# Second products as single matmuls between parts of the seven products, in a pattern of its own in each chunk

## The chip, the core and the metric

The kernel runs on one core of a Trainium2 chip. The metric is the device time of one execution in microseconds, and the median of several executions is compared. TensorE (PE) multiplies; VectorE (DVE), ScalarE (ACT) and GpSimd (POOL) do the element-wise work; SyncE (SP) issues most of the DMAs.

## The reference

Attention over a sliding window with a bias that grows with distance, and on its output, as rows of a 4608 x 512 matrix, a network of two layers with a squared ReLU between them.

```python
scores = scale * np.matmul(q, k.transpose(0, 1, 3, 2))       # 8 batches, 8 heads, 576 positions, 64 wide
mask = (rel >= 0) & (rel < 128)
scores = np.where(mask, scores + bias[None], -1000000000.0)
attn = np.exp(scores - max); attn = attn / (sum + 1e-09)
x = np.matmul(attn, v) as (4608, 512)
h = np.maximum(x @ w_in, 0.0)                                # w_in 512 x 2048
out = h * h @ w_out                                          # w_out 2048 x 512
```

## The kernel before

The 4608 rows of x go in nine chunks `c` of 512, and the 2048 hidden columns in 16 blocks `f` of 128. Matrix products keep their precision in three single-pass matmuls per operand pair: high part by high part, low by high, high by low.

The **first product** (x by `w_in`) is done plainly in chunks 0 and 1 (`gemm1`, line L224 of the profile). From chunk 2 on, two blocks of `f` at a time make one **step** `n` (eight steps a chunk, steps 16 to 71), by Strassen's scheme in Winograd's form: **seven products** M1, M5, M6, M2, M7, M3, M4 in this order (`seven`, `product`, L319), each of six matmuls 256 wide. M1, M6, M7 and M4 build up in one PSUM bank (`chain`), M5, M2 and M3 in another (`rest`). Between them stand **drains**, which copy or add a partial sum out of PSUM into `four`: s1, R, s2 and C21 on ACT, C11, C22 and C12 on DVE. A product waits for the drain of the one before it in its bank (`BEHIND`). Their left operands, `flow`, are sums of weights that were written to DRAM once, and come back by DMA two steps ahead; their right operands are parts of x (`xu`) and sums of such parts (`tees`). After a step, `squared` makes the hidden values on DVE (`r` or `spare`), ACT rounds them to the high part `hh`, and DVE subtracts for the low part `hl`.

The **second product** (h by `w_out`, `part`, L376) takes for each `f` four **blocks** `m`, of three matmuls 512 wide: weight high by `hh`, weight high by `hl`, weight low by `hh`. They build up in four banks `acc` over the 16 blocks of `f` of a chunk; then `give` copies a bank to SBUF (L382, ACT or DVE) and `send` writes it out (L386). The blocks of a step are worked off one step later, from a list `blocks`.

The attention of a later chunk runs beside this. Every second step ends with a **visit** (L719 and L732): PE multiplies the probabilities of one pair of heads with v, and makes the scores of the next pair. Then ACT copies the scores (L613, L620), DVE masks them and finds the maxima (L632, L636, L400), ACT exponentiates (L407), DVE sums (L414, L415), POOL normalizes (L419), DVE transposes in squares (L471), two DMA passes finish the transposition (`pp` to `way` and back), and POOL cuts the squares at the window (L484); the next visit waits for that. DVE, ACT and POOL also turn the visit's result into `xu`, `lows` and `tees` (L669, L699, L704).

`middle` writes PE's order by hand, step after step. The other engines' order is made by `Plan`: each piece of work has an engine, an assumed duration, what it comes after, and a due time; `run` goes through time, and among the pieces of an engine that are ready it takes the one due first. `start` plans the part before, chunks 0 and 1's attention and chunk 0's products, in the same way. The order of all queues is fixed when the kernel is built.

In `middle`, a step before the change runs so: M1, two blocks, M5, M6, two blocks, M2, M7, then two blocks in odd steps or one in even ones, M3, M4, in odd steps the visit, and then three blocks in odd steps or two in even ones (in the last chunk always two blocks, and no visits):

```python
counts = (2, 2, 2, 3 if n % 2 else 2) if n % 2 or n >= FULL - 8 else (2, 2, 1, 2)
for names, count in zip((("M1",), ("M5", "M6"), ("M2", "M7"), ("M3", "M4")), counts):
```

Of the kernel before, what the change touches and what calls it, by code (L numbers as in the profile page):

```python
# [22 lines left out]
NF = DF // 128  # L23
NCC = DM // 128
NCH = B * S // 512
# [6 lines left out]
WAIT = 0.1  # L32
# [7 lines left out]
FIRST = 19  # L40
# [23 lines left out]
class Kern:  # L64
# [249 lines left out]
    def product(self, n, i, to, name, start=False):  # L314
        todo = []
        for (wh, wl), (xh, xl) in zip(self.operand(n, i), self.halves(n // 8, name)):
            todo += [(wh, xh), (wl, xh), (wh, xl)]
        for k, (w, x) in enumerate(todo):
            self.nc.tensor.matmul(to, w, x, start=start and k == 0, stop=k == 5, skip_group_check=True)  # L319

    def seven(self, n):
        nc, four = self.nc, self.four
        one, two = slice(0, 256), slice(256, 512)
        add = lambda to, x: nc.vector.tensor_tensor(to, to, x, op=ALU.add)  # L324
        return {
            "M1": lambda: (self.chain(), self.product(n, 0, self.P, "B11", True)),
            "s1": lambda: nc.scalar.copy(four[0][:, one], self.P),
            "M5": lambda: (self.rest(), self.product(n, 1, self.R, "T1", True)),
            "R": lambda: nc.scalar.copy(four[1][:, two], self.R),
            "M6": lambda: self.product(n, 2, self.P, "T2"),  # L330
            "s2": lambda: nc.scalar.copy(four[0][:, two], self.P),
            "M2": lambda: self.product(n, 3, self.Q, "B21"),
            "C11": lambda: add(four[0][:, one], self.Q),
            "M7": lambda: self.product(n, 4, self.P, "T3"),
            "C22": lambda: add(four[1][:, two], self.P),
            "M3": lambda: self.product(n, 6, self.R, "B22"),
            "C12": lambda: add(four[0][:, two], self.R),
            "M4": lambda: self.product(n, 5, self.P, "T4"),
            "C21": lambda: nc.scalar.copy(four[1][:, one], self.P),  # L339
        }  # L340
# [27 lines left out]
    def part(self, c, f, m):  # L368
        if f == 0 and m == 0:
            self.acc = self.start_banks if c == 0 else [None] * 4  # L370
        if f == 0 and c:
            self.acc[m] = self.ac.tile([128, 512], F32, name="acc")
        hh, hl = self.h[c, f] if m < 3 else self.h.pop((c, f))
        wl, wh = self.block(1, f, m)
        for i, (w, h) in enumerate(((wh, hh), (wh, hl), (wl, hh))):
            self.nc.tensor.matmul(self.acc[m], w, h, start=(f == 0 and i == 0), stop=(f == NF - 1 and i == 2))  # L376
        if f == NF - 1:
            self.full[c, m] = self.acc[m]

    def give(self, c, m):  # L380
        o = self.out[c, m] = self.op.tile([128, 512], F32, name="o")
        (self.nc.scalar.copy if m % 2 else self.nc.vector.tensor_copy)(o, self.full.pop((c, m)))  # L382

    def send(self, c, m):
        out = self.outd[m * 128 : m * 128 + 128, 512 * c : 512 * c + 512]
        (self.nc.scalar if c == NCH - 1 and m == 3 else self.nc.sync).dma_start(out, self.out.pop((c, m)))  # L386
# [428 lines left out]
class Plan:  # L815


    def __init__(self, wait=WAIT, port=PORT):
        self.steps, self.count, self.wait, self.port = {}, {}, wait, port
# [12 lines left out]
    def run(self):  # L832
# [7 lines left out]
        while near:  # L840
# [16 lines left out]
            same = [r for r in ready if self.steps[r[2]][0] == on and r[0] <= first[0] + max(0.1, self.wait * span)]  # L857
# [132 lines left out]
ACT, DVE, POOL = "Activation", "DVE", "Pool"  # L990
SOFT = dict(M1=0.72, g=0.7, first=2.79, one=0.85, scores=0.75, two=0.65)
# [9 lines left out]
def middle(K, waiting):  # L1001
    P = Plan(0.7, ("t", "ws"))
# [13 lines left out]
    blocks = [(f, m) for f in (NF - 2, NF - 1) for m in range(4)]  # L1016

    def second(count):
        for _ in range(count):
            f, m = blocks.pop(0)  # L1020
            c, e = divmod(f, NF)
            after = [("hl", f)] if f >= NF else []
            if e == 0 and c:
                after.append(("give", c - 1, m))
            t = pe(("g", f, m), SOFT["g"], after, do(K.part, c, e, m), None, "hh" if m == 3 else None)
            if e == NF - 1:
                P.add(("give", c, m), ACT if m % 2 else DVE, 0.6, (("g", f, m),), t + 1.5, do(K.give, c, m), "o")
                P.add(("send", c, m), "SP", 0.8, (("give", c, m),), t + 8, do(K.send, c, m), None, "o", 1)

    def chain(q, s, V):  # L1030
        G, k = waiting[q].both[s], 2 * q + s
        n = lambda a, *m: (a, k, *m)
        for m in range(4):
            P.add(n("t", m), DVE, 0.22, (n("t", m - 1) if m else n("fold"),), V + 1.8 + 1.4 * s, do(G.top, m))
            P.add(n("e", m), ACT, 0.4, (n("t", m),) + ((n("e", m - 1),) if m else ()), V + 2 + 1.5 * s, do(G.exp, m))
        P.add(n("sum"), DVE, 0.42, (n("e", 3),), V + 2.4 + 1.4 * s, G.sums)
        P.add(n("norm"), POOL, 1.15, (n("sum"),), V + 2.4 + 1.4 * s, G.norm)
        turned(q, s, V + 2.5 + 1.4 * s, (n("norm"),))
# [11 lines left out]
    def visit(q):  # L1050
# [8 lines left out]
        if new and q + 1 < 4 * NCH:  # L1059
            for a, us in (("qk", 1.4), ("v", 0.9)):  # L1060
                fn = K.load_v if a == "v" else lambda c, p: (K.load_qk(c, p, 0), K.load_qk(c, p, 1))
                P.add((a, q + 1), "SP", us, ((a, q),) if (a, q) in P.steps else (), base + 12 if a == "qk" else base + 14, do(fn, *divmod(q + 1, 4)), a)
# [9 lines left out]
        if G.p < 2:  # L1072
# [3 lines left out]
            dues, reads, room = [16, 16.5, 16, 16.5, 18, 19], (0, 1, 2, 3), {0: ("o", None)}  # L1076
        else:
# [5 lines left out]
            late = [1.5, 3.4, 1.6, 2.6, 3.2, 1.5, 1.7, 3.4, 3.5, 8, 8.6, 7]  # L1083
            dues, reads, room = late if G.p == 3 else [16] * 5 + [18] * 6 + [16], (0, 1, 2, 3, 4, 11), {1: (None, "o")}
# [3 lines left out]
        if new:  # L1088
            for s in (0, 1):
# [4 lines left out]
                P.add(n("fill", s), POOL if late else "free", 0.4 * late, prior, base - 6, do(new.fill, s), "t")  # L1094
                P.add(
                    n("base", s), ACT, 1.2 if late else 0.58, (n("scores"), n("fill", s)) + behind("base"), V + s - 0.8,
                    do(new.base, s, False), None, ("one", "two") if s else None,
                )
                P.add(n("fold", s), DVE, 1.15 if late else 0.9, (n("base", s),) + behind("fold"), V + 0.3 + 2 * s, do(new.fold, s))
# [4 lines left out]
    for s in range(2):  # L1104
        turned(8, s, 4 + 3 * s, ())
    for n in range(NF, 2 * NF):
        g = K.gemm1(*divmod(n, NF))
        step = lambda g=g: next(g, None)
        if n == NF:
            second(2)  # L1110
        t = pe(("first", n), SOFT["first"], (), step, ("one", "two"))
        for i, (engine, us) in enumerate(((ACT, 0.6), (ACT, 0.6), (ACT, 0.6), (DVE, 0.66))):
            name = ("relu", "sq", "high", "hl")[i]
            P.add(
                (name, n), engine, us, ((("first", n),), (("relu", n),), (("sq", n),), (("high", n),))[i],
                t + (-800, 2.5, 3.2, 4)[i], step, (("r", "hh"), None, None, None)[i], (("one", "two"), None, None, "r")[i],
            )
        if (n - FIRST) % 4 == 0 and n >= FIRST:
            visit((n - FIRST) // 4 + 9)
        if n % 2:  # L1120
# [5 lines left out]
            d = t + 20 if j < 6 else t + 60  # L1126
# [7 lines left out]
            for name, engine, us, after in todo:  # L1134
                lag = {"a0": 2, "r0": 3, "s2": 1.5, "h0": 1.5, "l0": 1.5, "w0": 2.5}.get(name, 0)
# [5 lines left out]
        second(3 if n in (NF + 2, NF + 6, 2 * NF - 1) else 4)  # L1141
        blocks += [(n, m) for m in range(4)]
# [3 lines left out]
    def stream(n, i, t):  # L1146
        q = (2 * n - 7 - FIRST) // 4 + 9
        if n < FULL:
# [7 lines left out]
            P.add(("flow", n, i), "SP", 0.8, tuple(after), t + 17, do(K.stream, n, i), None, None, 0.5)  # L1156
# [5 lines left out]
    for n in range(NF, FULL):  # L1162
# [3 lines left out]
        counts = (2, 2, 2, 3 if n % 2 else 2) if n % 2 or n >= FULL - 8 else (2, 2, 1, 2)  # L1166
        if n % 2 and not V:
            counts = (2, 2, 2, 2)
        for names, count in zip((("M1",), ("M5", "M6"), ("M2", "M7"), ("M3", "M4")), counts):
            for m in names:  # L1170
                after = [("flow", n, PIECES.index(m))] + [(a, n) for a in BEHIND.get(m, ())]
                if j == 0:
                    after += needs(P, c, m)
                t = pe((m, n), SOFT["M1"], after, steps[m], {"M1": "one", "M5": "two"}.get(m))
# [9 lines left out]
            if names[0] == "M3" and V:  # L1184
                visit((2 * n + 1 - FIRST) // 4 + 9)
            second(count)
        for f in range(2):
# [6 lines left out]
            P.add(("sq", k), DVE, 0.65, after, now + 3 * f + 1.5, step, None if f else "r")  # L1194
            P.add(("high", k), ACT, 0.6, (("sq", k),), now + 3 * f + 2.2, step, "hh")
            P.add(("hl", k), DVE, 0.65, (("high", k),), now + 3 * f + 2.8, step, None, None if f else "r")
        blocks += [(2 * n + f, m) for f in range(2) for m in range(4)]
# [3 lines left out]
    K.ends = P.run()  # L1201

# [77 lines left out]
```

## Time and profile before

| | |
|---|---|
| median of three executions | 917.92 us (917.68 to 919.81) |
| the profiled execution | 919.04 us, span 917.3 us |
| PE busy | 905.9 us, 99% |
| weight loads busy | 803.1 us, 88% |
| DVE, ACT, POOL busy | 584.1, 466.8, 275.8 us |
| granted TensorE clock | 1.000 |

The span runs from the first to the last instruction. Rows give times from the start of the span. An engine's queue is worked off in order, so one waiting instruction holds all behind it. Matmuls are pipelined: the recorded length of one (0.39 for 512 wide) is longer than the spacing of starts (0.23), and the spacing is what adds up.

### The profile page before, as it was taken

What the parts mean: (1) busy time and instruction counts of PE and PEld (TensorE: products, weight loads), DVE (VectorE), ACT (ScalarE), POOL (GpSimd) and SP (SyncE); (2) the same over time, 40 slices, a digit from 0 to 9 for tenths busy, and PEclk for the clock granted to TensorE, in tenths of its full rate; (3) what the DMA queues carried; (4) which work ended last, traced back from release to release, by engine and by line L of the source; (5) the groups of instructions that cost most, each with busy time, mean ns of one, the idle gap of its engine ahead of it and who ended that gap; (6) DMA issues with size and microseconds to landing.
All of it is one profiled execution on the core that took longest, in us unless ns stands there. A gap on an engine that the chain in (4) does not pass through costs nothing.

```text
span 917.3 us, 23301 instructions
## 1 busy us (share of the span) xinstructions
PE 905.9 (99%) x8500; PEld 803.1 (88%) x8500; DVE 584.1 (64%) x1595; ACT 466.8 (51%) x1321; POOL 275.8 (30%) x339
## 2 busy tenths in 40 slices
PE   9999999999999999999999999999999999999998
PEld 5688888888889999999999999999999989989997
DVE  6999862776766666565756666667666565554333
ACT  7898663566555545444544544445444454433222
POOL 4213324665732223223322332233223232230000
PEclk9999999999999999999999999999999999999999
DMA  9985328668788888777877778777877776666541
GB/s 343 404 309 170 87 61 265 192 204 282 255 274 278 303 276 276 245 231 228 267 248 246 228 234 278 233 239 234 277 230 238 229 251 197 199 208 216 175 127 46
DMA packets 137425, 212.96 MB, mean 232 GB/s; under 512 B 15200, under 2 KB 49120, under 8 KB 137312
## 3 DMA queue, kind: packets, MB, share of 16 engines
q1 hardware_dynamic: 136880, 210.82, 71.5%
q8 instruction: 68, 1.11, 0.5%
q10 hardware_dynamic: 432, 0.66, 0.3%
q14 instruction: 45, 0.37, 0.1%
HBM read 170.52 MB, written 40.89 MB: 230 GB/s over the span
## 4 chain that ended last, share of the span: by engine, by line
PE 87%; DMA 7%; DVE 2%; ACT 1%; issue 1%; SPq 1%; POOL 1%; POOLq 0%; DVEq 0%; ACTq 0%
PE acc L376 41%; PE chain L319 16%; PE rest L319 12%; PE g L224 8%; PE s L719 4%; PE g L732 2%; DMA raw<-in_dram 2%; DMA qk<-in_dram 1%; PE s L732 1%; DMA ws<-both 1%; DMA flow<-ws 1%; PE at L496 1%; DMA way<-pp 1%; DMA wide<-in_dram 1%; POOL pp L484 1%
## 5 line engine op out<-in xcount | busy, mean ns | idle before, releaser
L376 PE MATMUL acc<-hh,w 128*128 128x512 f32 x1152 | 405.1, 397 | 0.0
L376 PEld LDWEIGHTS acc<-hh,w 128*128 128x128 f32 x1152 | 225.6, 196 | 38.5 <-issue 5.3
L376 PE MATMUL acc<-hl,w 128*128 128x512 f32 x576 | 226.3, 393 | 0.0
L484 POOL TENSOR_SCALAR_AFFINE_SELECT pp<-pp 128x512 f32<-128x512 f32 x128 | 101.8, 796 | 204.5 <-DMA pp<-way 73.9
L324 DVE TENSOR_TENSOR four<-four,rest 128x256 f32<-128x256 f32 x112 | 47.2, 422 | 178.1 <-PE rest L319 176.8
L419 POOL TENSOR_TENSOR t<-t,nm 128x512 f32<-128x512 f32 x64 | 73.3, 1147 | 280.5 <-DVE nm L415 241.1
L319 PEld LDWEIGHTS rest<-xu,flow 128*128 128x128 f32 x1008 | 146.3, 196 | 12.7 <-DVE four L324 0.5
L319 PE MATMUL chain<-tees,flow 128*128 128x256 f32 x1008 | 148.3, 283 | 0.3 <-POOL tees L669 0.3
L319 PE MATMUL rest<-xu,flow 128*128 128x256 f32 x1008 | 148.4, 284 | 0.0
L319 PEld LDWEIGHTS chain<-tees,flow 128*128 128x128 f32 x1008 | 133.1, 197 | 0.9 <-POOL tees L669 0.5
L339 ACT COPY four<-chain 128x256 f32<-128x256 f32 x56 | 20.9, 373 | 221.2 <-PE chain L319 221.2
L376 PEld LDWEIGHTS acc<-hl,w 128*128 128x128 f32 x576 | 112.6, 195 | 12.7 <-DVE hl L353 0.2
L407 ACT ACTIVATE t<-t,nm 128x128 f32<-128x128 f32 x256 | 101.1, 399 | 26.5 <-DVE nm L400 26.3
L224 PE MATMUL g<-xu,w 128*128 128x512 f32 x384 | 95.2, 397 | 0.7 <-ACT r L233 0.7
L224 PEld LDWEIGHTS g<-xu,w 128*128 128x128 f32 x384 | 76.3, 209 | 13.8 <-ACT r L233 1.2
L400 DVE CUSTOM_DVE_ANT_0 t<-t,cst 128x128 f32<-128x128 f32 x256 | 68.5, 314 | 1.2
L632 DVE COPY_PREDICATED t<-cst,s 64x256 f32<-64x256 int32 x100 | 44.6, 446 | 32.6 <-PE s L719 22.4
L471 DVE STREAM_TRANSPOSE pp<-t 128x512 f32<-128x512 f32 x64 | 45.4, 710 | 18.8 <-POOL t L419 18.0
L719 PE MATMUL s<-pp,v 64*64 64x128 f32 (+1 forms) x1792 | 52.7, 248 | 3.3 <-POOL pp L484 2.9
L319 PEld LDWEIGHTS chain<-xu,flow 128*128 128x128 f32 x336 | 48.7, 196 | 4.2
L319 PE MATMUL chain<-xu,flow 128*128 128x256 f32 x336 | 49.4, 284 | 0.0
L407 ACT ACTIVATION_READ_ACCUMULATOR t<-t,nm 128x1 f32 x256 | 49.0, 191 | 0.0
(104 smaller groups left out, 1129.6 us busy)
## 6 DMA issues: line engine op xcount, KB each, us to landing
flow<-ws SPq DMA_DIRECT2D x392, 256.0 KB, 4.0
raw<-in_dram SPq DMA_DIRECT2D x32, 512.0 KB, 8.7
way<-pp SPq DMA_DIRECT2D x256, 64.0 KB, 2.0
pp<-way SPq DMA_DIRECT2D x64, 256.0 KB, 3.6
qk<-in_dram SPq DMA_DIRECT2D x32, 320.0 KB, 4.5
v<-in_dram SPq DMA_DIRECT2D x32, 320.0 KB, 3.5
qk<-in_dram SPq DMA_DIRECT2D x38, 256.0 KB, 4.8
out_dram<-o SPq DMA_DIRECT2D x35, 256.0 KB, 3.1
```

The lines of the kernel that those rows point to most:

```text
L224: nc.tensor.matmul(g, w, xs[cc][:, part], start=i == 0, stop=i == 11)
L319: self.nc.tensor.matmul(to, w, x, start=start and k == 0, stop=k == 5, skip_group_check=True)
L324: add = lambda to, x: nc.vector.tensor_tensor(to, to, x, op=ALU.add)
L376: self.nc.tensor.matmul(self.acc[m], w, h, start=(f == 0 and i == 0), stop=(f == NF - 1 and i == 2))
L400: self.nc.vector.tensor_tensor_reduce(self.t[:, m], self.t[:, m], self.K.nrel(2 * self.p + m // 2), -0.125, BIG, ALU.add, ALU.min, self.nm ...
L407: return self.nc.scalar.activation(self.t[:, m], self.t[:, m], AF.Exp, bias=nm[:, 4 + m : 5 + m], scale=-1.0, accum_out=nm[:, m : m + 1],)
L419: self.nc.gpsimd.tensor_tensor(*(x.rearrange("p (j i) c -> p j i c", j=2) for x in (self.t, self.t)), self.rec.unsqueeze(3).to_broadcast([ ...
L471: nc.vector.transpose(squares.rearrange("p b m c -> p m b c"), self.t.rearrange("p m (b c) -> p m b c", c=32))
L484: nc.gpsimd.affine_select(to, self.own, pattern=[[-32 * sign, 4], [0, 4], [-sign, 32]], compare_op=op, fill=0.0, base=0, channel_multiplie ...
L632: nc.vector.copy_predicated(d, mask.unsqueeze(1).to_broadcast([64, 2, 2, 64]), e)
L719: yield self.nc.tensor.matmul(to, w, x, start=first and n < 2, stop=not first, skip_group_check=True)
L732: made = self.nc.tensor.matmul(to, w, x, start=not extra, stop=True, skip_group_check=True)
```

## The change

`product` and `part` get bounds `a`, `e`, so that a product or a block can be issued in pieces, and `middle` counts second products in single matmuls. A new function `weave` gives the order of a step, by chunk: chunk 2 keeps the old order; in chunks 3 to 8 M1, M5, M6, M2, M7 and M3 each have single second-product matmuls in or behind them, and M4 is followed by the visit (in odd steps up to chunk 7) and six single matmuls. All these steps hold 24 of them, eight blocks. Written as numbers of matmuls, the second products' in brackets, each of the six products goes so: chunk 3: 6 [3]; chunk 4: 3 [2] 3 [1]; chunk 5: 3 [1] 3 [2]; chunk 6: 2 [1] 2 [1] 2 [1]; chunk 7: 6 [2] and 6 [4] in turn; chunk 8: 1 [1] 2 [1] 1 [1] 2.

The last output tile is copied out of its bank in two halves, by ACT and by DVE, and each half is sent by a DMA of its own, over ACT's and SP's queue. The due times move into tables (`DUE`, `LAG`) with the values they had, and `Plan` gets a switch `mixed`, which is off.

```diff
-    def product(self, n, i, to, name, start=False):
+    def product(self, n, i, to, name, a, e, start=False):
...
-        for k, (w, x) in enumerate(todo):
+        for k, (w, x) in list(enumerate(todo))[a:e]:
...
-    def part(self, c, f, m):
+    def part(self, c, f, m, a=0, e=3):
...
-        for i, (w, h) in enumerate(((wh, hh), (wh, hl), (wl, hh))):
+        for i, (w, h) in list(enumerate(((wh, hh), (wh, hl), (wl, hh))))[a:e]:
...
     def give(self, c, m):
         o = self.out[c, m] = self.op.tile([128, 512], F32, name="o")
+        if (c, m) == (NCH - 1, 3):
+            x = self.full.pop((c, m))
+            self.nc.scalar.copy(o[:, 0:256], x[:, 0:256])
+            self.nc.vector.tensor_copy(o[:, 256:512], x[:, 256:512])
+            return
...
+        if (c, m) == (NCH - 1, 3):
+            self.nc.scalar.dma_start(out[:, 0:256], o[:, 0:256])
+            self.nc.sync.dma_start(out[:, 256:512], o[:, 256:512])
+            return
...
-    blocks = [(f, m) for f in (NF - 2, NF - 1) for m in range(4)]
+    blocks = [(f, m, i) for f in (NF - 2, NF - 1) for m in range(4) for i in range(3)]
...
+def weave(n, V):
+    M = lambda m, *cuts: [(m, a, b) for a, b in zip((0,) + cuts, cuts + (6,))]
+    visit = ["V"] if V else []
+    kind = n // 8 - 2
+    if kind == 0:
+        a, e = (6, 9) if V else (3, 6)
+        return M("M1") + [6] + M("M5") + M("M6") + [6] + M("M2") + M("M7") + [a] + M("M3") + M("M4") + visit + [e]
+    order = ("M1", "M5", "M6", "M2", "M7", "M3")
+    made = []
+    for i, m in enumerate(order):
+        if kind == 1:
+            made += M(m) + [3]
+        elif kind == 2:
+            x, y = M(m, 3)
+            made += [x, 2, y, 1]
+        elif kind == 3:
+            x, y = M(m, 3)
+            made += [x, 1, y, 2]
+        elif kind == 4:
+            x, y, z = M(m, 2, 4)
+            made += [x, 1, y, 1, z, 1]
+        elif kind == 5:
+            made += M(m) + [4 if i % 2 else 2]
+        else:
+            x, y, z, w = M(m, 1, 3, 4)
+            made += [x, 1, y, 1, z, 1, w]
+    return made + M("M4") + visit + [6]
```

What that makes of the queues, at three places. First PE in the first step of chunk 4, from M7 on (`tees_1662`) over M3 (`rest`) and M4 (`tees_1663`). Before:

```order
L319 MATMUL chain<-tees_1662,flow_4_1677 128x256 x6
L376 MATMUL acc<-hh,w_951 128x512
L376 MATMUL acc<-hl,w_951 128x512
L376 MATMUL acc<-hh,w_951 128x512
L319 MATMUL rest<-xu,flow_6_1679 128x256 x6
L319 MATMUL chain<-tees_1663,flow_5_1678 128x256 x6
L376 MATMUL acc<-hh,w_951 128x512
L376 MATMUL acc<-hl,w_951 128x512
```

And after:

```order
L319 MATMUL chain<-tees_1662,flow_4_1677 128x256 x3
L376 MATMUL acc<-hh,w_952 128x512
L376 MATMUL acc<-hl,w_952 128x512
L319 MATMUL chain<-tees_1662,flow_4_1677 128x256 x3
L376 MATMUL acc<-hh,w_952 128x512
L319 MATMUL rest<-xu,flow_6_1679 128x256 x3
L376 MATMUL acc<-hh,w_952 128x512
L376 MATMUL acc<-hl,w_952 128x512
L319 MATMUL rest<-xu,flow_6_1679 128x256 x3
L376 MATMUL acc<-hh,w_952 128x512
L319 MATMUL chain<-tees_1663,flow_5_1678 128x256 x6
```

The last `hl` shown is the first use of the low part that the step before made last; it stood behind M4 and stands between the halves of M3.

Second, DVE in the same step, from C11 (`four` with `rest`) over C22 (`four` with `chain`) to that `hl<-spare`. Before:

```order
L324 TENSOR_TENSOR four_1687<-four_1687,rest 128x256
L324 TENSOR_TENSOR four_1688<-four_1688,chain 128x256
L414 TENSOR_SCALAR nm<-nm 128x3x2
L415 RECIPROCAL nm<-nm 128x2x2
L353 TENSOR_TENSOR hl<-spare,hh 128x512
```

And after:

```order
L324 TENSOR_TENSOR four_1687<-four_1687,rest 128x256
L426 TENSOR_SCALAR nm<-nm 128x3x2
L427 RECIPROCAL nm<-nm 128x2x2
L681 TENSOR_TENSOR xu<-s,xu 128x256
L324 TENSOR_TENSOR four_1688<-four_1688,chain 128x256
L353 TENSOR_TENSOR hl<-spare,hh 128x512
```

The sum of the exponentials (`nm`) has moved ahead of C22, and `hl` still stands behind it.

Third, DVE in the first step of chunk 7, where C12 is the second `four` with `rest`. Before:

```order
L324 TENSOR_TENSOR four_1687<-four_1687,rest 128x256
L324 TENSOR_TENSOR four_1688<-four_1688,chain 128x256
L400 ISA t,nm<-t,cst 128x128
L400 ISA nm 128x1
L353 TENSOR_TENSOR hl<-spare,hh 128x512
L324 TENSOR_TENSOR four_1687<-four_1687,rest 128x256
L414 TENSOR_SCALAR nm<-nm 128x3x2
```

And after:

```order
L483 STREAM_TRANSPOSE pp<-t 128x4x4x32
L412 ISA t,nm<-t,cst 128x128
L412 ISA nm 128x1
L681 TENSOR_TENSOR xu<-s,xu 128x256
L426 TENSOR_SCALAR nm<-nm 128x3x2
L427 RECIPROCAL nm<-nm 128x2x2
L324 TENSOR_TENSOR four_1688<-four_1688,chain 128x256
L353 TENSOR_TENSOR hl<-spare,hh 128x512
```

The sum there stood behind C12 and stands ahead of C22.

More of the change, by code (lines that the diff above doesn't have):

```diff
@@ L1001, in middle @@
 def middle(K, waiting):
-    P = Plan(0.7, ("t", "ws"))
+    P = Plan(DUE["wait"][0], ("t", "ws"), DUE["wait"][1])
     for name, n in (
@@ L1165, in middle @@
         V = n % 2 and n < FULL - 8
[L1166 to L1174, printed above, removed]
+        for item in weave(n, V):
+            if item == "V":
+                visit((2 * n + 1 - FIRST) // 4 + 9)
+            elif isinstance(item, int):
+                second(item)
+            else:
+                m, a, e = item
+                after = []
+                if a == 0:
+                    after = [("flow", n, PIECES.index(m))] + [(x, n) for x in BEHIND.get(m, ())]
+                    if j == 0:
+                        after += needs(P, c, m)
+                t = pe(
+                    (m, n) if e == 6 else (m, n, a), SOFT["M1"] * (e - a) / 6, after, do(steps[m], a, e),
+                    {"M1": "one", "M5": "two"}.get(m) if a == 0 else None,
+                )
+                if e < 6:
+                    continue
                 for a, (engine, us, of) in DRAINS.items():
```

114 lines of the change are left out of this document (64 added, 50 removed).

## The prediction

> **What bounds the kernel now.** I read the page first: its head, the busy times (part 1) and the chain that ended last (part 4).
>
> ```profile
> span 917.3 us, 23301 instructions
> PE 905.9 (99%) x8500; PEld 803.1 (88%) x8500; DVE 584.1 (64%) x1595; ACT 466.8 (51%) x1321; POOL 275.8 (30%) x339
> PE 87%; DMA 7%; DVE 2%; ACT 1%; issue 1%; SPq 1%; POOL 1%; POOLq 0%; DVEq 0%; ACTq 0%
> ```
>
> TensorE (PE) is the bound: busy 905.9 of 917.3 us, and 87% of the chain. A busy PE need not be a PE at its peak, so next comes the busy time by stretch, for stretches of one chunk each (us, then PE, PEld, DVE, ACT, POOL, granted clock, DMA share, GB/s).
>
> ```profile
> 432.00:529.00 97.00, 97.00 (x1052) 88.82 (x1042) 60.91 (x181) 47.09 (x149) 27.17 (x38) 1.00 0.78 245
> 723.00:820.00 97.00, 95.96 (x976) 87.22 (x974) 60.66 (x177) 45.66 (x143) 27.37 (x33) 1.00 0.72 218
> ```
>
> A chunk costs 97 us, PE is never idle in chunk 4, and 1.04 us idle in chunk 7; the clock is full. So the time can move in three ways: by the pace at which matmuls follow each other, by waits that PE now has or will have, and at the two ends. The chain in order of time shows the pace (start, length, matmuls; "acc" are second products, 512 wide; "chain" and "rest" are the seven products, 256 wide).
>
> ```profile
> 411.56 1.40 PE acc L376 x6
> 416.50 0.72 PE chain L319 x6
> 417.22 0.69 PE acc L376 x3
> 419.35 1.39 PE acc L376 x6
> ```
>
> A product of six matmuls takes 0.72, so 0.120 each; six second-product matmuls take 1.39 to 1.40, three take 0.69, so 0.23 each. Single matmuls behind a product, from the timeline (the first number is the start):
>
> ```profile
> 419.19 0.39 PE L376 MATMUL acc<-hh,w 128*128 128x512 f32 x1
> 419.42 0.39 PE L376 MATMUL acc<-hl,w 128*128 128x512 f32 x1
> 419.64 0.63 PE L376 MATMUL acc<-hh,w 128*128 128x512 f32 x2
> 420.11 0.39 PE L376 MATMUL acc<-hl,w 128*128 128x512 f32 x1
> ```
>
> The starts are 0.23, 0.22 and then twice 0.235 apart: the first two after a product are a little shorter than those deep in a run. That is the small saving of two runs of three (2 x 0.69 = 1.38) against one run of six (1.39 to 1.40), 0.01 to 0.02 for one more switch. The rows round to 0.01; I take 8 ns, near the low end.
>
> **The change part by part.** *Counts.* Nothing is computed more or less: a step has 42 matmuls of the seven products and 24 of second products before (on the mean of an even and an odd step) and after. The bulk of 66 matmuls keeps its 42 x 0.120 + 24 x 0.23.
>
> *Pace.* Runs of second products in a step: four before. After, in chunks 3 to 8: 7, 13, 13, 19, 7 and 19, so 54 more a pattern round, times 8 steps 432 more switches from 256 to 512. Where a run keeps two or more matmuls the rows price it: chunks 3, 4, 5 and 7 gain three such runs a step, 4 x 3 x 8 x 8 ns = 0.8 us; chunks 6 and 8 lose three each, 0.4 back. Lone matmuls between two 256-wide ones, 48 a pattern round, 384 in all, stand nowhere in this trace. Between bounds: each saves 8 ns as a run does (384 x 8 ns = 3.1), or each costs 0.01 more, by the longest spacing in the rows above against the mean (3.8 the other way). The nearest row is the first 512 after a product, 0.23 against 0.235 deep in a run, so 2 ns each, 0.8 us. Sum of the pace: -1.2, bounds -3.5 and +3.4.
>
> *Second products around a visit.* Three blocks (9 matmuls) follow a visit before, two after, and even steps get eight blocks instead of seven. So the first M1 after a visit comes 3 x 0.23 = 0.7 earlier, and it needs the banks that ACT's copies of the scores give back.
>
> ```profile
> 432.60 1.29 ACT L620 COPY t<-g 64x256 f32<-64x256 f32 x4
> 432.60 0.51 PE L376 MATMUL acc<-hh,w 128*128 128x512 f32 x1
> 434.81 0.88 PE L319 MATMUL chain<-xu,flow 128*128 128x256 f32 x6
> ```
>
> The copies end at 433.89, M1 began at 434.81 and will begin at 434.11: 0.2 of cover is left, no wait. Priced at nothing.
>
> *Drains.* A product is copied out of its bank (s1, R, s2, C11 and so on) before the next one accumulates there. Between them stood one product and two blocks, 0.72 + 1.40; after, one product and three to six single matmuls, 0.72 + 0.7 to 1.4. The drain of M7 below starts 0.32 after its last matmul and takes 0.42, so even 1.42 covers it: nothing.
>
> *The last operand of the step before, at the start of a chunk.* In the first step of a chunk, ACT and DVE still work on the visit's results, and `hl` of the step before is late. Chunk 4:
>
> ```profile
> 440.47 0.88 PE L319 MATMUL chain<-tees,flow 128*128 128x256 f32 x6
> 441.39 0.42 DVE L324 TENSOR_TENSOR four<-four,chain 128x256 f32<-128x256 f32 x1 [0.23 <-PE chain L319]
> 439.96 0.62 ACT L351 CAST hh<-spare 128x512 fp32r<-128x512 f32 x1
> 440.78 0.42 ACT L407 ACTIVATE t<-t,nm 128x128 f32<-128x128 f32 x1
> 442.01 0.66 DVE L353 TENSOR_TENSOR hl<-spare,hh 128x512 fp32r<-128x512 f32 x1
> 443.55 0.39 PE L376 MATMUL acc<-hl,w 128*128 128x512 f32 x1
> ```
>
> `hl` is ready at 442.67 and first used at 443.55, in the sixth block, behind M4. The order shows that block between the halves of M3 now. By hand: M1 at 434.11, 1.42 a product with its three singles, M3 at 441.21, its first half 0.36, then `hh`, then `hl` at 441.80. DVE makes it after C22, which waits for M7 (two halves with two singles between them, last matmul at 440.86, C22 at 441.18): `hl` at 441.53 to 442.19. ACT puts the four last exponentials ahead of `hh`, so it may be 442.4. PE waits 0.45 to 0.65, I take 0.5. Chunk 3 needs `hl` at the end of M3, 442.16: 0.25. Chunk 6 at 441.92: 0.4. In chunk 5 both queues have the operand ahead of these waits, and in chunk 7 ACT makes `hh` early: nothing. Together +1.1, bounds 0 (queues keep up) and +2.5 (0.5 at all five). Behind the waiting matmul stand M3's second half and all that follows; nobody else is hurt. In chunk 3, where M2 is whole, `xu` may hold it by 0.2: +0.2.
>
> *The visit that waits.* The list of waits has one line that counts, and its shorter case lies in chunk 7:
>
> ```profile
> PE s L719 <- POOL pp L484: 2.9, 2, 2.1
> 733.26 0.42 DVE L324 TENSOR_TENSOR four<-four,rest 128x256 f32<-128x256 f32 x1
> 733.59 0.15 DVE L414 TENSOR_SCALAR nm<-nm 128x6 f32<-128x6 f32 x1
> 734.11 1.34 POOL L419 TENSOR_TENSOR t<-t,nm 128x512 f32<-128x512 f32 x1 [2.49 <-DVE nm L415]
> 743.47 2.06 POOL L484 TENSOR_SCALAR_AFFINE_SELECT pp<-pp 128x512 f32<-128x512 f32 x2 [3.79 <-DMA pp<-way]
> 744.41 0.33 PE L719 MATMUL s<-pp,v 64*64 64x64 f32 x2
> 745.59 0.89 PE L719 MATMUL s<-pp,v 64*64 64x64 f32 x29 [0.86 <-POOL pp L484]
> ```
>
> The visit starts at 744.41 and goes on at 745.59: 1.18 lost (an undisturbed one is not interrupted). The chain runs back over the transfer to POOL's `norm` at 734.11, and that to the sum on DVE, which stood behind C12, so behind M3. After the change the sum stands ahead of C22, as the order shows; M7's drain comes over 1 us before M3's. The chain gains more than the 1.18 lost: -1.2. What is late next is the read of `pp`, which then has some tenths in hand. Chunk 2's longer wait stands in the pattern that is kept.
>
> *The tail.* The last output tile is copied by ACT and DVE in halves, and sent over two queues.
>
> ```profile
> 913.19 0.40 PE L376 MATMUL acc<-hh,w 128*128 128x512 f32 x1
> 913.62 0.59 ACT L382 COPY o<-acc 128x512 f32<-128x512 f32 x1 [0.81 <-PE acc L376]
> 914.24 0.35 ACTq L386 DMA_DIRECT2D out_dram<-o  x1
> out_dram<-o ACTq DMA_DIRECT2D x1, 256.0 KB, 2.1
> way<-pp SPq DMA_DIRECT2D x256, 64.0 KB, 2.0
> ```
>
> A half copy takes 0.37 to 0.42 (C22's row) instead of 0.59; a transfer of a quarter of the size takes 2.0 against 2.1, so halving brings next to nothing. -0.2.
>
> *The start.* The diff touches nothing there, yet the order of DVE and ACT in it differs: among ready steps with equal due and start the planner takes the first of a Python set. PE's busy time there:
>
> ```profile
> 0.00:20.00 20.00, 18.48 (x123) 10.22 (x124) 11.57 (x67) 13.62 (x50) 7.92 (x12) 1.00 0.94 334
> 20.00:40.00 20.00, 19.06 (x210) 14.18 (x210) 18.48 (x50) 17.54 (x44) 7.05 (x8) 1.00 1.03 404
> 40.00:60.00 20.00, 18.47 (x123) 15.35 (x124) 19.60 (x44) 18.87 (x38) 2.37 (x2) 1.00 0.90 343
> ```
>
> 4.0 us idle in all, with DVE nearly full from 40 us on. The equal steps are alike, so I put 0, with half of that idle time, 2 us, to each side.
>
> *Sum.* -1.2 (pace) +1.1 +0.2 (operands) -1.2 (visit) -0.2 (tail) = -1.3. The profiled execution took 919.04 (span 917.3), 1.12 over the median of 917.92; with -1.3 it would take 917.7, and the median 916.6.
>
> **The rivals.** *Every switch saves.* If a lone matmul saves the 8 ns of a run, the pace brings 3.5 instead of 1.2: 914.3. For it: the first and the second matmul behind a product are both short. Against: the second is the shorter one, and a lone matmul has no second.
>
> *Weight loads get ahead.* If a 256-wide matmul is held by the load of the next weights, single 512-wide ones could let the loads run ahead. It would then last half of 0.233, 0.1165 instead of 0.120: 3.5 ns x 42 x 48 steps = 7.1 us in place of the 1.2: 910.7. Against: after six 512-wide matmuls, 1.39 us, the products still take 0.72. This is near a rule of the Trainium skill, "TensorE: Matmul & The Clock Gate", section "Back-to-back issue gap": spacing is set by weight load and matmul together, pipelined through a window 64 deep. By that rule a mixture would go faster than its parts; the trace shows no part of it yet.
>
> *Lone matmuls lose* (the slower side). If a 512-wide matmul between two short ones takes 0.24 instead of 0.23, 384 x 0.01 = 3.8 are lost and the gain of 1.2 is gone: 921.6. It decides from 7.5 ns each. For it: no row has this case. Against: at every switch, 256 to 512 and back, the spacing is that of the earlier matmul.
>
> *The clock falls.* Banks now change at nearly every matmul. At half the clock one chunk would take 97 us more, over 1010. Every stretch above has a clock of 1.00, with a change of bank every six matmuls. The Trainium skill, same page, section "A second HAM failure mode: psum-queue depth-cycling", says that cycling through banks makes PE idle in small pieces and the clock gate swing; it speaks against the change, and so far this trace does not bear it out.
>
> **How the numbers follow.** Less than 0.3% (2.75 us) cannot be told from no change. Forecast as summed, 914.8 to 919: 0.55, same. Every switch saves: 0.18, faster. Loads ahead: 0.06, faster. Lone matmuls lose: 0.10, slower. Clock: 0.01, slower. A start that falls out otherwise, by 2 us or more on top of the operands or the pace: 0.10, of it 0.04 faster, 0.04 same, 0.02 slower. Faster 0.28, same 0.59, slower 0.13. The range leaves out the loads that get ahead, the clock and the far end of the lone matmuls: 912.8 to 920.8. The likeliest case is 916.6.
>
> **What would show it.** Six-matmul products that stay at 0.72 when cut, in every chunk, and lone second-product matmuls at 0.23: the pace. A wait of `acc` for DVE's `hl` of 0.2 to 0.6 once in chunks 3, 4 and 6: the operands. No wait of `s` for POOL's `pp` in chunk 7. A last copy of 0.4. I am wrong if chunks with different patterns differ by more than 1 us in PE time, if new waits appear at several visits, or if PE's first long run begins much before or after 46 us.

## The result and the profile after

The changed kernel takes 931.07 us (median of four executions, 928.98 to 931.6) against 918.87 for the kernel before beside it (917.68 to 920.45): a ratio of 1.0126, 95% interval 1.0104 to 1.0147. It is slower; 916.6 had been forecast, 920.8 at most. The profiled execution took 931.26, with a span 12.2 us longer than before. Its page (head, busy time, the chain that ended last):

```profile
span 929.5 us, 23291 instructions
PE 911.2 (98%) x8496; PEld 804.8 (87%) x8500; DVE 586.8 (63%) x1596; ACT 462.8 (50%) x1321; POOL 277.5 (30%) x339
PE 84%; DMA 7%; DVE 4%; ACT 2%; POOL 1%; issue 1%; SPq 1%; DVEq 0%; POOLq 0%; ACTq 0%
```

PE is busy 5.3 us longer for the same matmuls and idle 6.9 us longer, and DVE's share of the chain has doubled. The list of waits (total, times, longest, us) says for whom:

```profile
PE s L731 <- POOL pp L496: 5.0, 1, 5.0
PE acc L376 <- DVE hl L353: 3.1, 4, 1.2
```

The first is the visit in chunk 2, where the order of PE's work is unchanged. The second did not exist before. To sort the 12.2 by place, I took the start of every visit and of every M1 from both traces. M1 to M1 is a step; "plain" is a step without a visit that is not the first of its chunk, with the old step put at 10.60 for its 24 second-product matmuls (chunk 8's, which has 24):

| | before | after |
|---|---|---|
| up to the visit in chunk 2 | 258.48 | 259.79 |
| from that visit to the next | 26.52 | 31.88 |
| first step of chunks 3, 4, 5, 6, 7, over the plain step of its chunk | 0, 0, 0, 0, 0.34 | 0.48, 1.67, 0, 1.58, 1.14 |
| plain step of chunks 3 to 8 | 10.60 | 10.677, 10.613, 10.620, 10.579, 10.683, 10.553 |

So 1.3 of the 12.2 arise in the start section, 5.4 at the one visit in chunk 2, 4.5 in the first steps of chunks, and about 1.0 in the pace. The visit in chunk 7 gives 1.1 back. The rest, 1.1, are small waits: 0.15 for a second late `hl` in chunk 4, and 0.9 at the last two visits of chunk 6.

*The visit in chunk 2.* POOL's rows before it, in the trace of before:

```profile
245.16 1.04 POOL L261 TENSOR_TENSOR both<-w 128x512 f32<-128x512 f32 x1
247.83 1.05 POOL L419 TENSOR_TENSOR t<-t,nm 128x512 f32<-128x512 f32 x1 [1.62 <-DVE nm L415]
248.83 1.49 POOL L261 TENSOR_TENSOR both<-w 128x512 f32<-128x512 f32 x1
```

and after:

```profile
246.56 2.29 POOL L261 TENSOR_TENSOR both<-w 128x512 f32<-128x512 f32 x2
248.93 0.87 POOL L268 TENSOR_TENSOR both<-both 128x256 f32<-128x256 f32 x1
251.94 1.34 POOL L431 TENSOR_TENSOR t<-t,nm 128x512 f32<-128x512 f32 x1 [2.15 <-ACT o L389]
```

The normalization that the visit waits for starts 4 us later. POOL's sums of weights, now two ahead of it instead of one, don't hold it: POOL is idle for 2.15 before it. It waits for DVE's sum of the exponentials (`nm`), behind the fourth of four row maxima. DVE's rows before:

```profile
242.75 0.26 DVE L400 CUSTOM_DVE_ANT_0 t<-t,cst 128x128 f32<-128x128 f32 x1
247.31 0.16 DVE L414 TENSOR_SCALAR nm<-nm 128x6 f32<-128x6 f32 x1 [0.41 <-ACT t L407]
```

and after:

```profile
250.26 0.28 DVE L412 CUSTOM_DVE_ANT_0 t<-t,cst 128x128 f32<-128x128 f32 x1
251.43 0.16 DVE L426 TENSOR_SCALAR nm<-nm 128x6 f32<-128x6 f32 x1 [0.27 <-ACT t L419]
```

Before, the first of the four maxima was made at 242.75. After, it isn't made there, and the fourth stands at 250.26, behind two drains and the hidden values `r`. What that does to PE, in the timeline:

```profile
265.12 1.55 PE L731 MATMUL s<-pp,v 64*64 64x64 f32 x30 [5.00 <-POOL pp L496]
```

and by stretch (length, then PE, PEld, DVE, ACT, POOL, granted clock, DMA share, GB/s):

```profile
262.00:264.00 2.00, 0.00 (x0) 0.00 (x0) 2.00 (x4) 0.00 (x0) 0.67 (x1) 0.90 1.01 367
266.00:267.00 1.00, 1.00 (x42) 1.00 (x38) 0.00 (x0) 0.00 (x0) 0.00 (x0) 0.50 0.97 344
270.00:272.00 2.00, 2.00 (x12) 1.55 (x8) 1.49 (x8) 1.53 (x6) 0.00 (x0) 0.90 1.02 376
```

PE stands still for 5.0 us. The granted clock falls to 0.50 at about 263.6, during the wait, and stays there until about 270.4. From the start of its first matmul to that of its last, the visit takes 10.07 instead of an undisturbed 2.52: 5.0 of the 7.55 are the wait, some 2.2 the clock (an estimate: at half the clock the 2.2 of work behind the wait take twice as long).

*The first step of chunk 4*, all four engines, at the place of which the prediction spoke:

```profile
450.10 0.50 PE L376 MATMUL acc<-hh,w 128*128 128x512 f32 x1
451.75 0.51 PE L376 MATMUL acc<-hl,w 128*128 128x512 f32 x1 [1.15 <-DVE hl L353]
449.56 0.16 DVE L426 TENSOR_SCALAR nm<-nm 128x6 f32<-128x6 f32 x1 [0.54 <-ACT t L419]
450.16 0.41 DVE L324 TENSOR_TENSOR four<-four,chain 128x256 f32<-128x256 f32 x1
450.49 1.21 DVE L353 TENSOR_TENSOR hl<-spare,hh 128x512 fp32r<-128x512 f32 x1
450.11 1.04 POOL L431 TENSOR_TENSOR t<-t,nm 128x512 f32<-128x512 f32 x1 [1.06 <-ACT hh L351]
```

`hl` is late at the very matmul that was forecast, but the next one starts 1.65 behind the last where 0.23 is usual: 1.42 lost, not 0.5. Two things stand in the rows that the forecast did not have. The sum (`nm`), which now stands ahead of C22, idles DVE 0.54 for ACT's last exponential. And `hl` itself takes 1.21, where it took 0.66: it lies beside the POOL normalization that this very sum releases. (The POOL row names ACT's `hh`, which also ended just before; the normalization needs the sum, whose reciprocal ended at 449.94.) No run put the sum back behind C22 with the pattern kept, so its 0.54 is read from the rows alone.

*The end.* The halves of the last tile:

```profile
925.82 0.37 ACT L386 COPY o<-acc 128x256 f32<-128x256 f32 x1 [0.82 <-PE acc L376]
926.22 0.42 DVE L387 COPY o<-acc 128x256 f32<-128x256 f32 x1 [0.41 <-ACT o L386]
926.68 0.33 SPq L396 DMA_DIRECT2D out_dram<-o  x1
```

DVE's half starts when ACT's has ended, not beside it. From the end of the last matmul to the end of the program it is 3.76, against 3.74 before.

### The profile page after: what moved, and what is told of

Read it like the earlier page. It is cut to its first block, busy times and chain, and to the rows that moved or that the text cites. A ratio compares the mean times of both kernels' runs of the same rounds, so it can differ in the third digit from the quotient of the medians.

```text
span 929.5 us, 23291 instructions
## 1 busy us (share of the span) xinstructions
PE 911.2 (98%) x8496; PEld 804.8 (87%) x8500; DVE 586.8 (63%) x1596; ACT 462.8 (50%) x1321; POOL 277.5 (30%) x339
## 4 chain that ended last, share of the span: by engine, by line
PE 84%; DMA 7%; DVE 4%; ACT 2%; POOL 1%; issue 1%; SPq 1%; DVEq 0%; POOLq 0%; ACTq 0%
PE acc L376 40%; PE chain L319 16%; PE rest L319 12%; PE g L224 7%; PE s L731 5%; PE g L744 2%; DMA raw<-in_dram 2%; DMA way<-pp 2%; PE s L744 1%; DMA pp<-way 1%; DMA wide<-in_dram 1%; ACT t L419 1%; POOL pp L496 1%; DMA qk<-in_dram 1%; PE at L508 1%
## 5 line engine op out<-in xcount | busy, mean ns | idle before, releaser
L376 PE MATMUL acc<-hh,w 128*128 128x512 f32 x1152 | 426.2, 398 | 0.1
L319 PEld LDWEIGHTS rest<-xu,flow 128*128 128x128 f32 x1008 | 168.0, 196 | 15.3
L319 PE MATMUL rest<-xu,flow 128*128 128x256 f32 x1008 | 175.0, 282 | 0.0
L319 PEld LDWEIGHTS chain<-tees,flow 128*128 128x128 f32 x1008 | 158.4, 196 | 12.5 <-POOL tees L681 0.5
L319 PE MATMUL chain<-tees,flow 128*128 128x256 f32 x1008 | 166.7, 283 | 0.3 <-POOL tees L681 0.3
L319 PEld LDWEIGHTS chain<-xu,flow 128*128 128x128 f32 x336 | 55.8, 195 | 6.3
L319 PE MATMUL chain<-xu,flow 128*128 128x256 f32 x336 | 58.3, 282 | 0.0
L353 DVE TENSOR_TENSOR hl<-spare,hh 128x512 fp32r<-128x512 f32 x56 | 47.8, 853 | 7.9 <-ACT hh L351 6.8
```

Source lines behind the costliest of these rows:

```text
L353: nc.vector.tensor_tensor(hl, r, hh.bitcast(F32), op=ALU.subtract)
```

## The experiments

The order of equal pieces is no property of the source: `Plan.run` takes the first of an unordered set, so two builds of the same file differ. In all runs below equal pieces are taken by name, so that the order is fixed. The kernel before, built anew without that beside each set, took 924.8, 923.8 and 924.3 there, and which order those builds had isn't recorded; so I compare the fixed runs with each other. The first four runs are one set, the next four (first steps, `hl`, first pattern) a second and the last three a third, each set on another chip; where a run is compared with one of another set, what the sets differ by, about 1 us by the medians just given, is in the difference too. A difference of medians stands with its 95% interval from resampling the executions (8 to 12 a kernel; the changed kernel in order b has only 4).

### Is the wait in chunk 2 the change's? Four runs

```diff
-            t, due, name = min(same, key=lambda r: (r[1], r[0]))
+            t, due, name = min(same, key=lambda r: (r[1], r[0], str(r[2])))                            # order a
+            t, due, name = min(same, key=lambda r: (r[1], r[0], r[2] == ("t", 25, 0), str(r[2])))      # order b
```

Before, order a: 

> The kernel before, with one addition: among pieces of work that the planner holds equal (same due time, same start) it now takes the first by name, not the first of an unordered set, so that the order of all queues is the same in every build. The equal pair that matters stands on VectorE at the end of chunk 1: a row maximum (t) of the 25th half visit, and a subtraction for the low parts. Here the maximum goes first. Theory A (the wait of 5.0 us in chunk 2 hangs on that pair, not on the change): the second product-of-probabilities in chunk 2 waits about 2.1 us as in the profile before, time 917 to 920. Rival B (the wait belongs to the change): the same, 917 to 920. This run is the base for the other three; the start section may differ by up to 2 us from the profile before.

Before, order b: 

> The same, with that one pair the other way round (the subtraction first); everything else is taken by name as in the run before. Theory A: the read of the probabilities in chunk 2 comes late, TensorE waits about 5.0 us instead of 2.1, and with the clock that falls behind it the time is 4 to 6 us above that of the run before, 922 to 925. Rival B: the wait stays at 2.1, same time within 1 us.

After, order a: 

> The changed kernel with equal pieces taken by name, and the maximum first in that pair. Theory A: the wait in chunk 2 is about 2.1, and what is left of the difference to the kernel before in the same order is the change's own: the chunk starts +6.4 (1.3, 1.9, 0.1, 1.6 and 1.7 in chunks 3 to 7), the pace +1.1, the visit in chunk 7 -1.1, chunk 8 and the tail -1.1, so 5 to 6 us above the first run of this set. Rival B: the wait stays at 5.0 and the difference is about 11 to 12 us.

After, order b: 

> The changed kernel with equal pieces taken by name and the subtraction first in that pair. Theory A: a wait of about 5.0 us in chunk 2 with a fallen clock, 10 to 12 us above the first run of this set, and 4 to 6 above the third. Rival B: as the third run, within 1 us.

Measured: 921.14, 925.58, 926.90, 929.34. One swapped pair of equal pieces costs the kernel before 4.4 us (2.9 to 5.9), and the changed kernel 2.4 (1.5 to 6.1). The visit in chunk 2 in orders a and b of the kernel before:

```profile
261.12 0.89 PE L719 MATMUL s<-pp,v 64*64 64x64 f32 x29 [1.27 <-POOL pp L484]
262.71 1.55 PE L719 MATMUL s<-pp,v 64*64 64x64 f32 x30 [4.66 <-POOL pp L484]
```

The long wait comes without the change and goes with it in place: A holds, B falls. The pair is the one in the rows above: that maximum stands at 243.80 in the first run and at 248.19, behind `r`, in the second, and up to that visit POOL's order in the changed kernel's first profile is the one of both runs in order b. The first run came out at 921.14 where 917 to 920 was expected, the second 0.6 above its range.

Inside order a the change costs 5.8 us (2.8 to 7.1), as A had it, though in part by luck. In the two profiled executions, whose spans are 6.8 apart, some 4.4 arise in the first steps of chunks, but 2.2 at the visit in chunk 2, which waits 1.97 with a fallen clock in the changed kernel. Up to there the queues of DVE, ACT, POOL and SP are the same in all six runs of the first two sets that have order a, and the visit waits 1.27, 1.97, 1.97, 0.86, 1.97 and 1.09 in them: that share is chance, not the change. The fourth run was over-estimated (8.2 above the first, not 10 to 12), for the same reason. In order a the first visit of the two kernels starts at 158.98 and 158.92, and over the four runs, whose start sections are planned alike, it lies anywhere from 157.59 to 158.98: of the 1.3 us in the start nothing can be put down to the change.

### Why is `hl` late at the chunk starts? Three runs

The normalization held behind `hl` at the chunk starts:

```diff
...
-        P.add(n("norm"), POOL, 1.15, (n("sum"),), V + DUE["norm"][s], G.norm)
+        held = (("hl", hold),) if s and hold else ()          # hold: the last hl of the chunk, at a chunk's last visit
+        P.add(n("norm"), POOL, 1.15, (n("sum"),) + held, V + DUE["norm"][s], G.norm)
...
```

> The changed kernel with the fixed order of equal pieces (base: its run in that order, 926.9 us), and at the start of each chunk GpSimd's second normalization held until VectorE has made the last hl of the chunk before. In the base that normalization starts just when hl does, and hl takes 1.2 us instead of 0.69. Theory C (the collision of VectorE and GpSimd is half of the late operand): hl takes 0.69 at the starts of chunks 3, 4 and 6, TensorE's wait for it falls by about 0.5 in each, 1.5 in all, 925 to 926. Rival D (hl is late only because of its place in ScalarE's and VectorE's queues): hl is not shorter or the wait doesn't fall, 927 within 1 us.

Chunk 4 in that run (PE, DVE, POOL):

```profile
447.33 0.51 PE L376 MATMUL acc<-hl,w 128*128 128x512 f32 x1 [0.63 <-DVE hl L353]
446.59 0.68 DVE L353 TENSOR_TENSOR hl<-spare,hh 128x512 fp32r<-128x512 f32 x1
447.82 1.05 POOL L431 TENSOR_TENSOR t<-t,nm 128x512 f32<-128x512 f32 x1
```

`hl` is back at 0.68, and the gap at the waiting matmul falls from 1.66 to 1.13 in chunk 4, and from 1.19 to 0.68 in chunk 6: the half microsecond of theory C at each (the base is the changed kernel in order a). In chunk 3 another POOL instruction (`tees`) took the normalization's place beside `hl`, which still took 1.22. The median is 924.75, 2.2 lower (3.8 lower to 1.0 higher), so the time alone would not prove it; the rows do. The other half of the lateness is the place in the queues (D).

The old order in each chunk's first step:

```diff
+    if n % 8 == 0:
+        return M("M1") + [6] + M("M5") + M("M6") + [6] + M("M2") + M("M7") + [3] + M("M3") + M("M4") + [9]
     order = ("M1", "M5", "M6", "M2", "M7", "M3")
```

> The changed kernel in the fixed order; the first step of each chunk from the third on has the old order of work again (six second-product matmuls behind M1, behind M6, three behind M7, nine behind M4), all other steps keep their new patterns. Theories C and D: the waits at the chunk starts (6.2 us in five chunks in the base) go nearly all, the visit in chunk 7 waits again by about 1 us, so 5 us less than the base, 921 to 923. Rival E (the switches between the two kinds of matmul cost the time, at chunk starts as elsewhere): the five first steps are a tenth of the switches, so less than 1 us falls, 926 to 927.

923.98, 2.9 lower (5.0 lower to 0.8 higher) where 5 was expected. No wait of `acc` for `hl` is left, and `hl` is ready 0.4 to 0.9 ahead of its use in every chunk; in chunk 7 the visit waits again, 0.8. In the profiled executions, whose spans are 3.5 apart, the first steps of chunks 3 to 8 give 4.2. The visit in chunk 2 gives another 2.6 by chance (it waits 0.86 at full clock, where the base's waits 1.97 and the clock falls). Waits at later places, visits for `pp` above all (0.7 and 0.9 in chunks 4 and 5), take 3.2 back, at places that wait in one run and not in another. The rows speak against E; the interval of the medians alone doesn't exclude it.

`hl` made early, the pattern kept:

```diff
+            early = 4 if n % 8 == 7 else 0
-            P.add(("high", k), ACT, 0.6, (("sq", k),), now + DUE["high"][f], step, "hh")
+            P.add(("high", k), ACT, 0.6, (("sq", k),), now + DUE["high"][f] - early, step, "hh")
```

(and the same for `hl`.) 

> The changed kernel in the fixed order with all its patterns; only the due times of the last hh and hl of each chunk are 4 us earlier, so that ScalarE and VectorE take them ahead of the exponentials, sums and squares of the visit. Theory D (place in the queues): the waits for hl at the starts of chunks 3, 4 and 6 go, 3 to 4 us less than the base, 923 to 924, and the visits keep their cover. Theory C alone: hl still collides with GpSimd here and there but is early enough, the same. Rival E: no change within 1 us. If the visits lose their cover, new waits of the scores for GpSimd, and nothing gained.

926.09, unchanged within the interval (2.4 lower to 2.1 higher). The waits for `hl` are gone, and these stand in their place:

```profile
PE rest L319 <- DVE xu L681: 2.8, 3, 1.6
PE s L731 <- POOL pp L496: 1.5, 2, 1.1
```

What `hl` was taken ahead of is needed just as soon: in chunks 5, 6 and 7 M2 waits for `xu`, an operand that DVE makes too, 2.8 in all. D's forecast of 3 to 4 us falls, though the place in the queue does decide whether `hl` is late. At a chunk's start DVE and ACT have so much due at once that an earlier place for this piece only moved the wait.

### What does the pattern cost? Four runs

First steps old, and all other steps of chunks 3 to 8 in chunk 8's pattern (`kind = min(n // 8 - 2, 1) * 6`):

> As the run before it, and all other steps of chunks 3 to 7 get the pattern of chunk 8 (1 [1] 2 [1] 1 [1] 2), which has the most switches. In the base a step of chunk 8 takes 10.553 us against 10.60 in the kernel before, while chunk 3's pattern costs 0.07 a step more than before. Theory F (the pace depends on where the single matmuls stand, and that pattern saves 0.045 a step): 35 steps, 1.6 us below the kernel before at that place, and some 2.5 below the run with the five patterns, 918 to 921. Rival E (each switch costs): slower than the run with the five patterns, 922 or more.

920.27, 3.7 below the run with the five patterns (1.2 to 6.9). Plain steps now take 10.55 in all of them. Chunk 4:

```profile
444.61 0.39 PE L376 MATMUL acc<-hh,w 128*128 128x512 f32 x1
444.84 0.28 PE L319 MATMUL chain<-xu,flow 128*128 128x256 f32 x1
444.96 0.39 PE L376 MATMUL acc<-hh,w 128*128 128x512 f32 x1
445.19 0.40 PE L319 MATMUL chain<-xu,flow 128*128 128x256 f32 x2
445.43 0.40 PE L376 MATMUL acc<-hl,w 128*128 128x512 f32 x1
```

A lone 512-wide matmul takes 0.233 from start to start (756 of them, median), neither more nor less than deep in a run. The 256-wide ones take 0.117 alone (294), 0.238 in twos and 0.354 in threes, where six take 0.719, 0.1198 each. With 34 in such short runs in a step that saves about 0.05 (an estimate from these medians), which is where the 0.047 a step lies.

That kernel with a hold on the weight sums in chunk 2, the kernel before with the same hold, and the former with chunk 3's pattern, 6 [3], in place of chunk 8's:

```diff
-            todo += [(f"r{k}", POOL, 1.3, after) for k in range(2)] + ...
+            todo += [(f"r{k}", POOL, 1.3, after + ((("norm", 25),) if j == 7 else ())) for k in range(2)] + ...
```

> The run with the first steps in the old order and chunk 8's pattern everywhere else (its median 920.3 us), and in addition the sums of weights of the last group (GpSimd's both from w) are held until GpSimd has normalized the second half of the visit in chunk 2. In the run before they stand ahead of that, VectorE's maximum beside them takes 1.15 instead of 0.28, and TensorE waits 2.0 us in chunk 2. Theory G (that pair of engines again makes the wait in chunk 2): the wait falls by about 1 us, 918 to 920 and faster than the kernel before. Rival H (the wait is set by the two DMA passes behind it): within 0.5 us of 920.3, the same wait of 2.0.

> The kernel before with equal pieces taken by name, and the same hold of the weight sums in chunk 2. Nothing of the change is in it. Theory G: 1 us less than the kernel before in the same order, whose wait there was 1.3 to 2.1; so 1 to 2.5 us above the run beside it, which has the new patterns. Rival H: no change against 921, the same wait.

> As the first run of this set, but with chunk 3's pattern, 6 [3], in all steps of chunks 3 to 8 other than the first of each chunk, in place of chunk 8's. Theory F (the pace depends on the pattern): chunk 3's steps took 0.07 us more than the old ones and chunk 8's 0.045 less, so 0.115 x 42 steps = 4.8 us slower than the first run of this set. Rival E (each switch costs): this one has fewer switches, so it is the faster. Rival I (the 0.07 was the neighbourhood of the visits, not the pattern): within 1 us of it.

922.12, 922.65 and 926.71. The hold did nothing for the visit in chunk 2, which waits 2.0 in each of the first two, as H had it. (Both times lie above H's 920.3 and 921; visits wait in other chunks, 0.9 and 2.0 in chunks 4 and 5 of the one, 1.2 and 0.9 in chunks 4 and 7 of the other.) The normalization came 0.4 earlier against the visit's start (11.0 ahead of it, not 10.65), but the write behind it didn't: on SP's queue it stands behind the first half's read, which waits for the first half's transfer (read at 249.98, write at 250.39). Chunk 3's pattern is 4.6 slower than chunk 8's (2.5 to 5.8), with plain steps of 10.64 to 10.69 against 10.553: the pattern sets the pace (F), the number of switches does not (E falls), nor does the neighbourhood of the visits (I).

No version is shown to beat the kernel before. The best pattern is 0.5 us below it in the same set (1.6 below to 1.2 above), and its two runs differ by more than that, through visits that wait now in one chunk, now in another.

## Why the prediction was wrong, point by point

- **"Chunk 2's longer wait stands in the pattern that is kept"**: this failed, +5.4 in the profile. The text had seen that equal pieces are ordered by a set, and confined it to the start section ("I put 0, with half of that idle time, 2 us, to each side"). The same toss, at a pair on DVE in chunk 2's first step, decides when the sum is made and POOL can normalize. It is no effect of the change.
- **Operands at the chunk starts, +1.1 and +0.2, bounds to 2.5**: the term that was mis-sized, and the change's main cost. 0.25, 0.5, 0, 0.4 and 0 were forecast, 0.48, 1.67, 0, 1.58 and 1.14 measured, 4.9 in all and beyond the upper bound. Place and time of need were right: 450.33 in chunk 4, against 450.22 when the forecast is moved by 8.42 to this trace's M1. The time of supply was not. It was counted from the end of M7 through C22, though the quoted order has the sum ahead of C22, and that sum waits for ACT (C22 starts at 450.16 against 449.60, moved likewise); and `hl` was priced at the 0.66 of a trace in which it seldom lay beside POOL. In chunk 7 `hl` took 1.51, with POOL's normalization ahead of it for 0.97, and was 1.0 late where nothing was forecast.
- **The visit in chunk 7, -1.2**: right. It is no longer interrupted, and its step is 1.1 shorter:

```profile
758.51 0.90 PE L731 MATMUL s<-pp,v 64*64 64x64 f32 x32
```

 The same move of the sum that wins this 1.1 sends POOL into `hl` at the chunk starts. The forecast booked the gain and not the price.
- **Pace, -1.2, bounds -3.5 and +3.4**: +1.0, inside the bounds with the wrong sign. Lone 512-wide matmuls at 0.23: right. Products at 0.719 when whole, and 0.357 for half: right. What failed is the 8 ns for each run of three: such a run took 0.690 between two products before, and 0.701 in chunk 3's pattern. The gain lies elsewhere, in the 256-wide matmuls that run in ones, twos and threes, 1 to 3 ns each. Why a run of three loses its 11 ns there isn't settled.
- **Tail, -0.2**: 0. Two halves of one tile were copied one behind the other.
- **M1 after the visit, and the drains, nothing**: right but for chunk 7, where M1 of the second step lost some 0.3 to a late drain (C21) in the changed kernel in fixed order.
- **The rivals**: the clock did not fall from changing banks (1.00 through chunk 8, where they change at every matmul or second one); it fell where PE stood still. Loads that get ahead: 0.117 to 0.119 for 0.120, only in short runs, and whether by the loads no run shows. "Lone matmuls lose", the slower side, forecast 921.6 by a mechanism that isn't there. The slower side that came, DVE and POOL in each other's way behind a moved sum, was not among the rivals.

## What to carry to other kernels

A reordering on the engine that is full is paid for on the others: before trusting a price for a piece that moves, look which instruction of a neighbouring engine will now lie beside it, and what a moved piece releases there. Where a planner breaks ties by the order of a set, fix that first: here one toss was worth 4.4 us and the change 5.8 (chance included), and a comparison of single builds mixed up the two. Interleaving matmuls of two widths one by one costs nothing by itself: here the best pattern gained 0.4% of a step, and the one of whole products and runs of three lost 0.7%.

## What the runs showed of the hardware

*A subtraction on VectorE and an instruction on GpSimd that reads SBUF exclude each other.* In the changed kernel 22 of the 112 `hl` of chunks 2 to 8 started while POOL was in an instruction that reads SBUF. Each ended 0.53 to 0.55 after POOL's ended, whatever its own start. That makes 1.2 for most, and 1.51 in chunk 7; all four that PE waits for at chunk starts lay beside a normalization (1.19, 1.21, 1.21 and 1.51). Where `hl` came first it took its 0.66 to 0.69, and POOL's normalization 1.31 to 1.55 instead of 1.05. The kernel before had 5 such cases, none of them the operand that a chunk's start needs, so its trace held rows that could have warned: four `hl` at 1.14 to 1.22, and one at 0.87, beside POOL's cutting of the squares. The Trainium skill, "SBUF — State Buffer", section "Who interferes with whom", says just this: a VectorE instruction with two inputs in SBUF and a GpSimd one that reads SBUF share a read path, the first holds it for the whole instruction, and the other is fully blocked. The trace agrees.

*A short stop can halve the clock.* The visit in chunk 2 waits 1.97 us both in the changed kernel in order a and in the first run with chunk 8's pattern. The stretch behind that wait in the one (the granted clock is the third number from the end):

```profile
262.00:263.00 1.00, 1.00 (x33) 1.00 (x29) 0.65 (x2) 0.00 (x0) 0.00 (x0) 0.50 1.05 377
```

and in the other:

```profile
261.00:262.00 1.00, 1.00 (x64) 1.00 (x60) 0.68 (x2) 0.00 (x0) 0.00 (x0) 1.00 0.98 340
```

In the one the clock is halved for some 3.4 us from 261.3 on (the stretches of 1 us from 261 have 0.66, 0.50, 0.50 and 0.64) and the visit takes 6.29, in the other it stays and the visit takes 4.81: the same wait costs 1.5 us more or not. The Trainium skill, "TensorE: Matmul & The Clock Gate", section "What's actually happening", puts the fall after an idle window of some 3.4 us, whose phase is free. The waits of 4.66 to 5.53 agree with that. The shorter ones differ: 1.97 at this visit was enough in three runs and not in two others, and 2.89 was not in one.
